# A batch's gate and row-sum rounds gathered in one place, three exponentials a group for four, and a third score buffer

## Chip, core and metric

The kernel runs on one core of one Trainium2 chip. The metric is the device time of one execution in microseconds (us). Five things work side by side: TensorE (PE, matmuls; its weight loads are PEld), VectorE (DVE), ScalarE (ACT), GpSimd (POOL), and SyncE (SP), which here only issues DMA transfers. Each engine takes its instructions strictly in the order in which the program lists them.

## What is computed

Attention with capped scores, and behind it a layer of eight experts to which tokens are assigned greedily:

```python
# q, k, v: 8 batches x 12 heads x 448 x 64, float32; cap = 30
scores = cap * np.tanh(scale * (q @ k.T) / cap)
attn = exp(scores - max); attn = attn / (sum(attn) + 1e-09)
x = (attn @ v), heads side by side: 3584 x 768
logits = x @ w_gate                       # 8 experts, each takes 448 tokens,
...                                       # in order of falling logit
out[mask] = np.maximum(x[mask] @ w1[e], 0.0) @ w2[e]
```

The change lies in the attention alone.

## The kernel before, in words

Attention goes through N = 24 groups, g = 0 to 23. A group is four heads of one batch, so a batch b is three groups, m = 0, 1, 2 with g = 3b + m; they are called G0, G1 and G2 of the batch here. A group has seven rows r = 0 to 6 of key positions. For each row there is

- a score block (`qk`, L148), four matmuls of 64x64 weights and 448 columns into a pair of PSUM banks, which ACT reads with Tanh (L159) into a tile `e`;
- an exponential on the tile of Tanh results, in place (L164). Rows are taken together for it: 0 and 1, 2 and 3, 4 and 5, and 6 alone (`GRP`, L134). It is issued behind the Tanh of the row after its last (`wait`, L161);
- a value block (`avq`, L196), four matmuls that add `e` times the values into the accumulator `psA`, one pair of banks for a whole group. The value blocks of group g run while the score blocks of g+1 do. When all seven are done, DVE copies `psA` into `xT` (`av_out`, L210), and only then may the first value block of the next group write `psA` again.

On the side DVE turns the keys and queries of the next group (`tr`, L133: tiles `tk`, `tq`), adds up a group's exponentials into a tile `es` (`esum`, L170: three adds, a fourth for G2), and turns the attention output of two batches before (`turn`, L271). POOL adds the two halves of `es` for G0 and G1 (`halves`, L356 and L357: a copy of one element, `pin`, which holds it until a certain add of DVE is done, and the add), and scales the turned output by the row sums (`scale`, L278: `xw<-x,R`), which SP then stores. `es` has four buffers, `xw` and `x` two.

For each batch b there are three rounds of small matmuls (`rnd`, L219; 32 rows of result each), which form the gate logits from `xT` and the row sums from `es`, side by side in one bank. They are made for batch b-1 during batch b: R0 in G0, R1 in G1, R2 in G2. Behind R2 DVE copies the banks out (`logit_in`, L256 and L258) and forms the reciprocals of the sums (`sums`, L261 and L262), which POOL spreads into `R` (L264, four copies). In G0 of the next batch PE turns the logits (`ltr`, L290) and DVE finishes them (`logit`, L301 to L309), and POOL adds up the heads (`heads`, L326). In the first batch there are four rounds, since its first group is laid out differently.

The order of all this is written out by hand: the body of the loop over g (L364 to L398) and, for PE, the strings `ORDER`, `EARLY`, `BEFORE` and `FINAL` (L348 to L351), where Q3 is the score block of row 3, A3 the value block of row 3 of the group before. No scheduler reorders it. PSUM has eight banks: two pairs for scores (`psS`), two single banks (`psM`) for rounds, turns and the like, and the pair `psA`.

After the attention come the search for the first expert's tokens and the experts' matmuls, which the change does not touch.

Of the kernel before, what the change touches and what calls it, by code (L numbers as in the profile page):

```python
# [8 lines left out]
PSUM=bass.MemoryType.PSUM  # L9
# [8 lines left out]
def attention(nc, tc, c1, xp, pM, ep, nl, pT, q, k, v, cap, w_gate, xs, L1, ident, on_logits, on_turn, NDEF, setup, mark):  # L18
# [29 lines left out]
    with ExitStack() as ctx:  # L48
# [5 lines left out]
        pS=ctx.enter_context(tc.tile_pool(name="pS",bufs=2,space=PSUM))  # L54

# [31 lines left out]
        ips=pM.tile([128,512],F32,name="psM")  # L87
# [46 lines left out]
        GRP=((0,1),(2,3),(4,5),(6,)); LOC={r:(gi,n) for gi,rs in enumerate(GRP) for n,r in enumerate(rs)}  # L134
# [5 lines left out]
        def qk(g,r):  # L140
            gi,n=LOC[r]
            if n==0: eh[g,gi]=ep.tile([128,len(GRP[gi]),2,S],F32,name=f"e{gi}")
            ps=pS.tile([128,2,512],F32,name="psS")
            if g:
                for o in range(2):
                    for h in range(2):
                        hp=slice(h*64,h*64+64)
                        nc.tensor.matmul(ps[o*64:o*64+64,h,:S],tks[g,0][hp,o,r*64:r*64+64],tks[g,1][hp,o,:],start=True,stop=True)  # L148
            elif r<6:
                o,u=divmod(r,3)  # L150
                for h in range(2):
# [10 lines left out]
            if g==N-1 and gi>=2: e=ev(g,r)  # L162
            elif n<len(GRP[gi])-1: return
            act=lambda: nc.scalar.activation(e,e,AF.Exp,scale=sr[1],bias=bias)  # L164
            if g==N-1 and gi>=2: act()
            else: wait.append(act)
        def esum(g,what):
            if not 0<=g<N: return
            if what=='e1': es_t[g]=es.tile([128,2,2,S],F32,name="es",bufs=4)
            t=es_t[g]; add=lambda o,a,b: nc.vector.tensor_tensor(o,a,b,op=ALU.add)  # L170
            if g==0 and what in ('e1','e2'):
                o=int(what[1])-1
                add(t[:,o],ex(g,o,0),ex(g,o,1)); add(t[:,o],t[:,o],ex(g,o,2))
            elif g==0:
                e=ev(g,6)
                for o in range(2):
                    w=slice(64*(1-o),128-64*o)
                    add(t[w,o],t[w,o],e[w])
# [62 lines left out]
        def logit_v(b,of,t,under):  # L241
# [3 lines left out]
            ps=pM.tile([128,512],F32,name="psM")  # L245
# [113 lines left out]
        def rounds(bb,m,n):  # L359
            rnd(bb,*RNO[bb>0][n])  # L360
            if m==2:
                logit_in(bb)
                if bb<B-NDEF: sums(bb)
        for g in range(N):  # L364
# [7 lines left out]
            order=g>=G2; first=bb==0; old=bb-1 if m==0 and 0<=bb-1<B-NDEF else None  # L372
            qk(g,0)
            if old is not None: ltr(old)
            if m==0 and bb>=0: rounds(bb,m,"R0")
            qk(g,1)
            av_out(g-2)
            if g and (m or g<G2): avq(g-1,0)
# [5 lines left out]
            two=(0,1) if m==1 else (1,0)
            tr(g+1,two[0] if order else 0)
            if order: tr(g+1,two[1])
            if m==1 and bb>0: on_logits(bb-1)
            for w in ('e2','r') if g==1 else ('e2','r6'): esum(g-1,w)
            if g>1 and not HELD(g-1): esum(g-1,'r0')
            if last: halves(N-2,None)  # L390
            if not order: tr(g+1,1)
            for t in (EARLY[g] if g<2 else FINAL if last else BEFORE if g==N-2 else ORDER[m]).split():
                if t[0]=='R': bb>=0 and rounds(bb,m,t)
# [11 lines left out]
        two=pS.tile([128,2,512],F32,name="psS")  # L405
# [22 lines left out]
class Routing:  # L428
# [198 lines left out]
    def search(s,wp,turned=()):  # L627
# [7 lines left out]
        if turned:  # L635
# [3 lines left out]
            post=lambda: s.flips(s.pm.tile([128,512],F32,name="psM"))  # L639
# [461 lines left out]
def full(nc,tc,q,k,v,cap,wg,w1,w2,out):  # L1101
    with ExitStack() as ctx:
# [10 lines left out]
        pM=xctx.enter_context(tc.tile_pool(name="pM",bufs=2,space=PSUM,side="right"))  # L1113
        r.psum=lambda: pM.tile([128,512],F32,name="psM")
# [13 lines left out]
        deferred,tail=attention(nc,tc,cp,xp,pM,ep,nl,pT,q,k,v,cap,wg,xs,L1,ident,on_logits,on_turn,NDEF,(r.indices,r.setup),r.mark)  # L1128
# [37 lines left out]
```

## Time and profile before

| | |
|---|---|
| time, median of 3 runs | 857.54 us (857.45 to 857.86) |
| the profiled execution | 858.0 us, of which its span 856.2 us |
| granted TensorE clock | 0.999 of full speed |
| PE busy | 840.2 us, 98% of the span |
| DVE, ACT, POOL busy | 580.4, 572.4, 462.5 us |
| a batch of the attention in its steady part, mean | 35.39 us |

The profiled execution is one run, recorded by the hardware; its span is the stretch from its first to its last instruction. Busy time is that in which an engine has an instruction under way; a busy PE may still stand still between matmuls, so pauses there are found from the starts of its rows. In rows of the timeline, neighbours of one kind are merged (x24 means 24 records), and a bracket names what ended the idle time ahead of the row. A float32 matmul leaves two records, so a block of four matmuls shows as x8.

### The profile page before, as it was taken

Reading aid. Unit: us, or ns where it says so; the run is one execution under the profiler, and the core shown is the slowest. Engines: PE = TensorE matmul, PEld = TensorE weight load, DVE = VectorE, ACT = ScalarE, POOL = GpSimd, SP = SyncE. Lnnn points to the kernel's source line nnn. Section 1 sums busy time; section 2 is a strip of 40 time slices with the busy share of each in tenths; the row PEclk is TensorE's granted clock in tenths of the full one; section 3 lists DMA queues with packets and bytes.
Section 4 is the critical chain, followed back from the end, with each engine's and each line's share of the span. In section 5 each row is a group of like instructions: output and inputs, shape, how many; then the busy total and the mean of one; then the engine's idle time right before and its main releaser. Section 6 shows DMA issues by size and latency. Waiting matters only on the chain.

```text
span 856.2 us, 17676 instructions
## 1 busy us (share of the span) xinstructions
PE 840.2 (98%) x6109; PEld 614.5 (72%) x6109; DVE 580.4 (68%) x1907; ACT 572.4 (67%) x832; POOL 462.5 (54%) x637
## 2 busy tenths in 40 slices
PE   8999999999999998999999999999999999999997
PEld 5333333333333357889889989989899899999997
DVE  3878899999989778667777777777757780230110
ACT  6999999999999753562764755737727725525521
POOL 8203336346333235573673864856856856837931
PEclk9999999999999999999999999999999999999999
DMA  8999999888995107716706917927928828838601
GB/s 126 137 142 148 157 158 156 159 160 158 154 152 125 23 2 226 229 36 189 222 16 193 311 42 209 317 58 207 308 56 211 288 65 232 257 118 234 202 10 56
DMA packets 364249, 133.70 MB, mean 156 GB/s; under 512 B 290592, under 2 KB 357472, under 8 KB 364160
## 3 DMA queue, kind: packets, MB, share of 16 engines
q1 hardware_dynamic: 354656, 102.27, 55.5%
q0 software_dynamic: 4656, 22.02, 7.5%
q10 hardware_dynamic: 4848, 8.29, 2.9%
q8 instruction: 48, 0.79, 0.4%
q14 instruction: 41, 0.34, 0.1%
HBM read 94.40 MB, written 30.08 MB: 145 GB/s over the span
## 4 chain that ended last, share of the span: by engine, by line
PE 76%; issue 7%; DVE 5%; SPq 5%; DMA 4%; POOL 2%; ACT 1%; POOLq 0%; ACTq 0%; DVEq 0%
PE psH L1002 25%; PE psH L1033 20%; PE psA L196 13%; PE psS L148 12%; SPq L83 3%; PE psM L219 2%; DVE es L170 2%; DMA xg<-xs,idx 1%; DVE cmpD L605 1%; POOL w2l L884 1%; DMA k<-in_k_dram 1%; DMA w1r<-in_moe_w_dram 1%; PE psX L826 1%; PE psM L290 1%; SPq L867 1%
## 5 line engine op out<-in xcount | busy, mean ns | idle before, releaser
L1033 PE MATMUL psH<-w2h,hh 128*128 128x384 f32 x896 | 235.3, 340 | 0.0
L1033 PE MATMUL psH<-w2l,hh 128*128 128x384 f32 x512 | 166.5, 340 | 0.5 <-POOL gap L882 0.5
L1033 PEld LDWEIGHTS psH<-w2h,hh 128*128 128x128 f32 x896 | 161.8, 188 | 0.3
L164 ACT ACTIVATE e<-e,bias 128x1792 f32<-128x1792 f32 (+1 forms) x97 | 158.5, 1636 | 0.1
L159 ACT ACTIVATE e<-psS 128x896 f32<-128x896 f32 x168 | 150.5, 956 | 11.1 <-PE psS L148 7.1
L1002 PE MATMUL psH<-xgh,w1h 128*128 128x448 f32 x384 | 143.2, 373 | 0.3 <-ACT xgh L962 0.3
L1002 PE MATMUL psH<-xgh,w1l 128*128 128x448 f32 x384 | 141.5, 369 | 0.0
L148 PE MATMUL psS<-tq,tk 64*64 64x448 f32 x1288 | 139.3, 538 | 1.1 <-ACT e L159 1.1
L884 POOL TENSOR_TENSOR w2l<-w2r,w2h 128x768 fp32r<-128x768 f32 x64 | 118.1, 1846 | 37.5 <-ACT w2h L880 30.5
L1002 PE MATMUL psH<-xgl,w1h 128*128 128x448 f32 x384 | 136.8, 369 | 0.0
L196 PE MATMUL psA<-e,nv 64*64 64x448 f32 x1232 | 131.9, 539 | 1.0 <-DVE xT L210 1.0
L884 POOL TENSOR_TENSOR w1l<-w1r,w1h 128x768 fp32r<-128x768 f32 x62 | 114.2, 1843 | 19.7 <-ACT w1h L880 15.3
L148 PEld LDWEIGHTS psS<-tq,tk 64*64 64x64 f32 x1288 | 47.5, 132 | 75.4 <-issue 47.0
L196 PEld LDWEIGHTS psA<-e,nv 64*64 64x64 f32 x1232 | 44.8, 133 | 73.8 <-issue 64.3
L1033 PEld LDWEIGHTS psH<-w2l,hh 128*128 128x128 f32 x512 | 95.6, 188 | 1.5 <-POOL gap L882 1.4
L1008 ACT ACTIVATE hh<-psH 128x448 fp32r<-128x448 f32 x64 | 34.8, 544 | 86.4 <-PE psH L1002 80.1
L1010 DVE SCALAR_TENSOR_TENSOR hh<-psH,hh 128x64 fp32r<-128x64 f32 (+1 forms) x128 | 44.0, 386 | 67.8 <-ACT hh L1008 66.7
L1039 ACT ACTIVATE on<-psH 128x384 f32<-128x384 f32 x48 | 23.4, 487 | 88.5 <-PE psH L1033 82.5
L170 DVE TENSOR_TENSOR es<-es,e 128x896 f32<-128x896 f32 (+2 forms) x48 | 77.7, 1619 | 2.5
L909 POOL DMA_INDIRECT xg<-xs,idx x32 | 34.3, 1073 | 81.2 <-DVE zz L774 64.8
L1002 PEld LDWEIGHTS psH<-xgh,w1h 128*128 128x128 f32 x384 | 72.5, 189 | 5.8 <-ACT xgh L962 0.5
L1002 PEld LDWEIGHTS psH<-xgh,w1l 128*128 128x128 f32 x384 | 72.3, 188 | 5.3
(390 smaller groups left out, 1339.1 us busy)
## 6 DMA issues: line engine op xcount, KB each, us to landing
w1r<-in_moe_w_dram SPq DMA_DIRECT2D x128, 192.0 KB, 4.7
w2r<-in_moe_w_dram SPq DMA_DIRECT2D x64, 384.0 KB, 6.5
k<-in_k_dram SPq DMA_DIRECT2D x92, 112.0 KB, 3.8
q<-in_q_dram SPq DMA_DIRECT2D x92, 112.0 KB, 4.0
nv<-in_v_dram SPq DMA_DIRECT2D x88, 112.0 KB, 3.3
xs<-xw SPq DMA_DIRECT2D x72, 112.0 KB, 2.6
xz<-pl ACTq DMA_DIRECT2D x18, 384.0 KB, 3.3
xs<-xn SPq DMA_DIRECT2D x1, 1344.0 KB, 6.5
```

Of the source, the lines that this page charges most:

```text
L83: (nc.scalar if first and a else nc.sync).dma_start(z[w:w+32,lo*NB:hi*NB,:],src[b,h0+2*t+lo:h0+2*t+hi,:,a*32:a*32+32].rearrange("h (k s) d ...
L148: nc.tensor.matmul(ps[o*64:o*64+64,h,:S],tks[g,0][hp,o,r*64:r*64+64],tks[g,1][hp,o,:],start=True,stop=True)
L159: nc.scalar.activation(ev(g,r),ps[:,:,:S],AF.Tanh,scale=sr[0])
L164: act=lambda: nc.scalar.activation(e,e,AF.Exp,scale=sr[1],bias=bias)
L170: t=es_t[g]; add=lambda o,a,b: nc.vector.tensor_tensor(o,a,b,op=ALU.add)
L196: nc.tensor.matmul(avp[g,o][h*64:h*64+64,:S],z[hp,r,h,:],ev(g,r)[hp,h,:],start=r==0,stop=r==6)
L884: (eng or nc.gpsimd).tensor_tensor(view(l),r,view(h).bitcast(F32),op=ALU.subtract)
L909: g=nc.gpsimd.indirect_dma_start(out=row(j,n),out_offset=None,in_=xs,in_offset=bass.IndirectOffsetOnAxis(ap=res[p][0][:n,j:j+1],axis=0))
L1002: nc.tensor.matmul(ps[:,:C],a[:,c,:],b[:,c,:],start=(m==0),stop=(m==DC*3-1)); m+=1
L1008: nc.scalar.activation(h[:,:C],ps[:,:C],AF.Relu)
L1010: nc.vector.scalar_tensor_tensor(h[:,d:d+b-a],ps[:,a:b],0.0,h[:,a:b].bitcast(F32),op0=ALU.max,op1=ALU.subtract)
L1033: nc.tensor.matmul(ps[:,:HD],h[:,f,a:a+128],spl[p,2,hf,f//2][w][:,f%2,:],start=(m==0),stop=(m==nm-1))
```

## The change

1. The exponentials of a group are taken in three parts, rows 0 to 2, 3 and 4, 5 and 6.
2. `es` is summed by five adds of 896 columns (`p`, `q`, `s`: rows 0+1+2 into one half, 3+4+5+6 into the other) in place of two of 1792 and one of 896. The sixth, for G2, joins the halves as before.
3. The three rounds stand together at the end of G1 of the next batch, with `logit_in` and `sums` behind them; `halves` runs in G2 and G0 and no longer in G1 and G2.
4. Scores, rounds, turns and logits share one ring of three pairs of banks (`two_banks`), where there were two pairs for scores and two single banks for the rest.
5. The order is one string a group, in which letters stand for the side work too: c is `av_out`, T `ltr`, l `logit`, t `turn`, `scale` and `tr`, s and a the adds, p the first two adds of the group itself, o the first half of the routing's proposals, i `logit_in` and `sums`. A5- and A6- are value blocks left over from the group before the last.

```diff
+        def two_banks():
+            two_banks.n+=1
+            return pS.tile([128,2,512],F32,name="psS") if two_banks.n%3 else pM.tile([128,2,512],F32,name="psM")
...
-        GRP=((0,1),(2,3),(4,5),(6,)); LOC={r:(gi,n) for gi,rs in enumerate(GRP) for n,r in enumerate(rs)}
+        GRP=((0,1,2),(3,4),(5,6)); LOC={r:(gi,n) for gi,rs in enumerate(GRP) for n,r in enumerate(rs)}
...
-            ps=pS.tile([128,2,512],F32,name="psS")
+            ps=two_banks()
...
-            elif what=='e1': add(t,eh[g,0],eh[g,1])
-            elif what=='e2': add(t,t,eh[g,2])
-            else:
-                r=int(what[1])
-                add(t[:,0],t[:,0],ev(g,r) if r else t[:,1])
+            if what=='p': add(t[:,0],ev(g,0),ev(g,1)); add(t[:,0],t[:,0],ev(g,2))
+            elif what=='q': add(t[:,1],ev(g,3),ev(g,4))
+            elif what=='r': add(t[:,0],t[:,0],t[:,1])
+            else:
+                add(t[:,1],t[:,1],ev(g,5))
+                if g: add(t[:,1],t[:,1],ev(g,6))
...
-                    if b not in bank: bank[b]=pM.tile([128,512],F32,name="psM")
+                    if b not in misc:
+                        two=two_banks()
+                        for o,z in enumerate((misc,side)): z[b]=two[:,o]
...
+        ORDER=["Q0 c T l t s a A0 Q1 Q2 Q3 A1 A2 Q4 A3 Q5 A4 A5 A6 p Q6",
+               "Q0 c t s a o Q1 A0 A1 Q2 Q3 A2 A3 Q4 A4 Q5 R0 R1 R2 p i Q6",
+               "Q0 A5- A6- c t s a Q1 Q2 Q3 A0 A1 Q4 A2 Q5 A3 A4 A5 A6 p Q6"]
...
-            if m: halves(g-4+m,g-1)
+            if m!=1: halves(g-2,g-1)
...
+                elif t=='s':
+                    esum(g-1,'q'); esum(g-1,'s')
+                elif t=='a':
+                    if not HELD(g-1): esum(g-1,'r')
```

What becomes of the order is seen on three engines, each time in the fifth batch. On PE, before, this is the middle of G1, with round R1 between two score blocks and a value block (L148 is a score block, L196 a value block, `e_...` the exponentials it reads, L219 a round):

```order
L196 MATMUL psA<-e_1840,nv 64x448 x4
L148 MATMUL psS<-tq,tk 64x448 x4
L219 MATMUL psM<-xT,gw 32x448 x2
L219 MATMUL psM<-es,ones 32x448 x2
L196 MATMUL psA<-e_1840,nv 64x448 x4
L148 MATMUL psS<-tq,tk 64x448 x8
```

And this is the end of the same G1 in the changed kernel (score blocks are L153 now, value blocks L199, rounds L224), up to the first blocks of G2:

```order
L199 MATMUL psA<-e_1893,nv 64x448 x4
L153 MATMUL psS<-tq,tk 64x448 x4
L224 MATMUL psS<-xT,gw 32x448 x2
L224 MATMUL psS<-es,ones 32x448 x2
L224 MATMUL psS<-xT,gw 32x448 x2
L224 MATMUL psS<-es,ones 32x448 x4
L224 MATMUL psS<-xT,gw 32x448 x2
L153 MATMUL psM<-tq,tk 64x448 x4
L153 MATMUL psS<-tq,tk 64x448 x4
L199 MATMUL psA<-e_1919,nv 64x448 x8
```

All twelve matmuls of the rounds stand in a row now, ahead of the last score block of G1, and the value blocks of rows 5 and 6 (`e_1919`) have moved behind them, into G2.

On DVE, before, this is the stretch from the last adds of G1 through G2 (L210 is the copy of `psA`, L271 and L133 the three transposes, L256 to L262 `logit_in` and `sums`):

```order
L170 TENSOR_TENSOR es<-e_1972,e_2008 128x1792
L210 COPY xT<-psA 128x896
L271 STREAM_TRANSPOSE x_2116<-xT 128x896
L133 STREAM_TRANSPOSE tq<-q 128x896
L133 STREAM_TRANSPOSE tk<-k 128x896
L170 TENSOR_TENSOR es<-es,e_2030 128x1792
L170 TENSOR_TENSOR es<-es,e_2052 128x896
L256 COPY lg<-psM 128x448
L258 TENSOR_TENSOR lg<-lg,psM 64x448
L261 STREAM_TRANSPOSE lgt<-lg 64x448
L262 RECIPROCAL rec<-lgt 64x84
L170 TENSOR_TENSOR es<-e_2089,e_2126 128x1792
```

The same stretch in the changed kernel (adds are L175, the copy of `psA` L213, `logit_in` and `sums` L261 to L267):

```order
L175 TENSOR_TENSOR es<-e_1967 128x896
L175 TENSOR_TENSOR es<-es,e_1967 128x896
L261 COPY lg<-psS 128x448
L263 TENSOR_TENSOR lg<-lg,psS 64x448
L266 STREAM_TRANSPOSE lgt<-lg 64x448
L267 RECIPROCAL rec<-lgt 64x84
L213 COPY xT<-psA 128x896
L276 STREAM_TRANSPOSE x_2114<-xT 128x896
L138 STREAM_TRANSPOSE tq<-q 128x896
L138 STREAM_TRANSPOSE tk<-k 128x896
L175 TENSOR_TENSOR es<-e_2008 128x896
L175 TENSOR_TENSOR es<-es,e_2034 128x896 x2
```

`logit_in` and `sums` have moved ahead of the copy of `psA` and of the transposes, and each long add has become two short ones.

On POOL, before, this is one batch from the `scale` of G0 on (L278 `scale`, L356 and L357 `halves`, L264 the four copies into `R`, L326 `heads`):

```order
L278 TENSOR_TENSOR xw<-x_1879,R_1788 128x14x2x32
L356 COPY pin<-es 1x1
L357 TENSOR_TENSOR es<-es 128x896
L278 TENSOR_TENSOR xw<-x_1998,R_1788 128x14x2x32
L356 COPY pin<-es 1x1
L357 TENSOR_TENSOR es<-es 128x896
L278 TENSOR_TENSOR xw<-x_2116,R_1788 128x14x2x32
L264 COPY R_2167<-rec 32x84 x4
L326 TENSOR_TENSOR lt_2251<-lt_2251 112x4x48
```

In the changed kernel, from the `scale` of G1 on:

```order
L283 TENSOR_TENSOR xw<-x_1976,R_1686 128x14x2x32
L269 COPY R_2064<-rec 32x84 x4
L362 COPY pin<-es 1x1
L363 TENSOR_TENSOR es<-es 128x896
L283 TENSOR_TENSOR xw<-x_2114,R_1686 128x14x2x32
L362 COPY pin<-es 1x1
L363 TENSOR_TENSOR es<-es 128x896
L331 TENSOR_TENSOR lt_2235<-lt_2235 112x4x48
```

The copies into `R` stand ahead of the first `halves` and of the `scale` of G2 now, and the second `halves` (that of G1) ahead of `heads` and of the `scale` of the next G0.

## Rows read from the trace of the kernel before

**Rows 1.** The windows view, five whole batches: busy time of each engine.

```profile
78.83:255.80 176.97, 176.97 (x1825) 66.56 (x1821) 164.95 (x176) 174.84 (x166) 80.58 (x90) 1.00 0.97 156
```

**Rows 2.** The timeline of PE (start, length): first score blocks of batches, one run of blocks.

```profile
78.83 0.93 PE L148 MATMUL psS<-tq,tk 64*64 64x448 f32 x8
...
147.25 2.44 PE L196 MATMUL psA<-e,nv 64*64 64x448 f32 x24
149.50 0.93 PE L148 MATMUL psS<-tq,tk 64*64 64x448 f32 x8
```

**Rows 3.** The timeline of PE, G0 and G1 of the fifth batch: side work.

```profile
150.36 0.65 PE L290 MATMUL psM<-ident,lg 128*112 128x128 f32 x4
150.94 0.57 PE L219 MATMUL psM<-xT,gw 128*32 128x448 f32 x2
...
164.77 0.57 PE L219 MATMUL psM<-xT,gw 128*32 128x448 f32 x2
...
165.66 0.98 PE L196 MATMUL psA<-e,nv 64*64 64x448 f32 x8
```

**Rows 4.** The timeline of DVE, fifth batch, from `logit_in` to G1.

```profile
145.55 0.62 DVE L256 COPY lg<-psM 128x448 f32<-128x448 f32 x1
...
148.23 2.02 DVE L170 TENSOR_TENSOR es<-e,e 128x1792 f32<-128x1792 f32 x1
150.18 1.08 DVE L210 COPY xT<-psA 128x896 f32<-128x896 f32 x1
...
152.10 1.10 DVE L271 STREAM_TRANSPOSE x<-xT 128x896 f32<-128x896 f32 x1
...
155.11 3.71 DVE L170 TENSOR_TENSOR es<-es,e 128x1792 f32<-128x1792 f32 x2
158.86 1.09 DVE L170 TENSOR_TENSOR es<-es 128x896 f32<-128x896 f32 x1
159.87 2.02 DVE L170 TENSOR_TENSOR es<-e,e 128x1792 f32<-128x1792 f32 x1
161.90 1.09 DVE L210 COPY xT<-psA 128x896 f32<-128x896 f32 x1
...
177.49 3.18 DVE L170 TENSOR_TENSOR es<-es,e 128x1792 f32<-128x1792 f32 x2
```

**Rows 5.** The timeline of ACT, fifth batch: exponential, Tanh, short exponential.

```profile
161.04 1.82 ACT L164 ACTIVATE e<-e,bias 128x1792 f32<-128x1792 f32 x1
162.72 0.95 ACT L159 ACTIVATE e<-psS 128x896 f32<-128x896 f32 x1
163.52 1.08 ACT L164 ACTIVATE e<-e,bias 128x896 f32<-128x896 f32 x1
```

**Rows 6.** The timeline of DVE and POOL in G2 of the last batch, two on one memory.

```profile
284.00 1.98 DVE L170 TENSOR_TENSOR es<-es,e 128x1792 f32<-128x1792 f32 x1
286.09 2.42 DVE L170 TENSOR_TENSOR es<-es,e 128x896 f32<-128x896 f32 x1
284.22 3.35 POOL L278 TENSOR_TENSOR xw<-x,R 128x896 f32<-128x896 f32 x1 [11.06 <-issue]
```

**Rows 7.** The timeline of POOL, fifth batch, from the copies into `R` on.

```profile
148.34 2.90 POOL L264 COPY R<-rec 32x84 f32<-32x84 f32 x4 [5.78 <-DVE rec L262]
...
152.33 1.39 POOL L326 TENSOR_TENSOR lt<-lt 112x192 f32<-112x192 f32 x3 [1.09 <-DVE lt L309]
...
154.01 1.74 POOL L278 TENSOR_TENSOR xw<-x,R 128x896 f32<-128x896 f32 x1
...
162.09 2.09 POOL L357 TENSOR_TENSOR es<-es 128x896 f32<-128x896 f32 x1
```

**Rows 8.** The timeline of DVE, then PE, second batch: loads arrive late.

```profile
47.81 1.11 DVE L133 STREAM_TRANSPOSE tq<-q 128x896 f32<-128x896 f32 x1 [3.60 <-DMA q<-in_q_dram]
...
56.00 1.08 DVE L210 COPY xT<-psA 128x896 f32<-128x896 f32 x1
...
57.14 0.98 PE L196 MATMUL psA<-e,nv 64*64 64x448 f32 x8 [0.55 <-DVE xT L210]
```

More of the change, by code (lines that the diff above doesn't have):

```diff
@@ L86, in attention @@
         nc.scalar.activation(tb,ident[:,0:1],AF.Tanh)
-        ips=pM.tile([128,512],F32,name="psM")
+        ips=pT.tile([128,2,512],F32,name="psA",bufs=1)[:,0]
         def idle(n):
@@ L168, in esum @@
             if not 0<=g<N: return
[L169 to L178, printed above, removed]
-            elif what=='e1': add(t,eh[g,0],eh[g,1])
-            elif what=='e2': add(t,t,eh[g,2])
-            else:
-                r=int(what[1])
-                add(t[:,0],t[:,0],ev(g,r) if r else t[:,1])
+            if what=='p': es_t[g]=es.tile([128,2,2,S],F32,name="es",bufs=4)
+            t=es_t[g]; add=lambda o,x,y: nc.vector.tensor_tensor(o,x,y,op=ALU.add)
+            if what=='p': add(t[:,0],ev(g,0),ev(g,1)); add(t[:,0],t[:,0],ev(g,2))
+            elif what=='q': add(t[:,1],ev(g,3),ev(g,4))
+            elif what=='r': add(t[:,0],t[:,0],t[:,1])
+            else:
+                add(t[:,1],t[:,1],ev(g,5))
+                if g: add(t[:,1],t[:,1],ev(g,6))
+                else:
+                    e=ev(g,6)
+                    for o in range(2):
+                        w=slice(64*(1-o),128-64*o)
+                        add(t[w,o],t[w,o],e[w])
         avp={}; pair=[None]
@@ L371, in attention @@
             last=g==N-1
[L372 to L378, printed above, removed]
-            stored()
-            if m: halves(g-4+m,g-1)
-            if old is not None: logit(old); heads(old)
-            if m==0 and bb>1: on_turn(bb-2)
-            turn(b-2,m); scale(b-2,m)
@@ L384, in attention @@
[L384 to L393, printed above, removed]
+            old=bb-1 if m==0 and 0<=bb-1<B-NDEF else None
@@ new lines, in attention @@
+            two=(0,1) if m==1 else (1,0)
+            stored()
+            if m!=1: halves(g-2,g-1)
+            for t in (EARLY[g] if g<G2 else FINAL if last else ORDER[m]).split():
+                if t[0]=='Q': qk(g,int(t[1]))
+                elif t[0]=='A': avq(g-1-(t[-1]=='-'),int(t[1]))
+                elif t[0]=='R': bb>=0 and rnd(bb,*RNO[bb>0][t])
+                elif t=='c': av_out(g-2)
+                elif t=='T': old is not None and ltr(old)
+                elif t=='l':
+                    if old is not None: logit(old); heads(old)
+                    if bb>1: on_turn(bb-2)
+                elif t=='t':
+                    turn(b-2,m); scale(b-2,m)
+                    for part in two: tr(g+1,part)
+                elif t in 'kv': tr(g+1,t=='v')
+                elif t=='s':
+                    esum(g-1,'q'); esum(g-1,'s')
+                elif t=='a':
+                    if not HELD(g-1): esum(g-1,'r')
+                    if last: halves(N-2,None)
+                elif t=='o': bb>0 and on_logits(bb-1)
+                elif t=='i':
+                    if bb>=0:
+                        logit_in(bb)
+                        if bb<B-NDEF: sums(bb)
+                elif t=='p': esum(g,'p')
@@ L404, in attention @@
         LAST=[RA,RB]
-        two=pS.tile([128,2,512],F32,name="psS")
+        two=two_banks()
+        misc[b]=two[:,1]
         part_v(two[:,0],0,1)
```

43 lines of the change are left out of this document (18 added, 25 removed).

## The prediction

> **What bounds the kernel now.** I read the windows view first, then the timelines of PE, ACT, DVE and POOL over one batch. In five steady batches PE is busy all of 176.97 us, ACT 174.84, DVE 164.95, at a granted clock of 1.00 [rows 1]: a batch takes 35.39 us, PE has no free time, ACT lacks 1% of being the bound, DVE 7%.
>
> PE's 35.39 can be added up. A block of four matmuls takes 0.75 (three blocks in 149.50 - 147.25 = 2.25) [rows 2], so the 42 score and value blocks take 31.5. Going over to side work costs 0.11 (150.36 - 149.50 - 0.75), `ltr` 0.58 (150.94 - 150.36), a round 0.89 (165.66 - 164.77), and the block behind it shows 0.98 for 0.93, so 0.05 for going back [rows 2, 3]. G0 pays 0.11 + 0.58 + 0.89 + 0.05 = 1.63 for `ltr` and R0, G1 and G2 1.05 each: 3.73 a batch, 35.2 in all. The reader is to see that PE does not pause here, so a gain must shorten PE's own list, and a loss must make PE wait. What can make it wait is the copy of `psA`: the value block at 57.14 starts 0.06 after that copy ends (56.00 + 1.08), with 0.55 of PE standing still [rows 8].
>
> **The change part by part.** *PE.* Each round holds 0.75 of pure matmul time like a block; the other 0.14 of its 0.89 I count as part of going back. Three rounds in a row cost 0.11 + 3 x 0.75 + 0.14 + 0.05 = 2.55, `ltr` alone 0.11 + 0.58 + 0.05 = 0.74: 3.29 for 3.73, 0.44 saved a batch. PE alone would need 31.5 + 3.29 = 34.8.
>
> *ACT.* A Tanh takes 0.80 (163.52 - 162.72), an exponential of 1792 columns 1.68 (162.72 - 161.04), one of 896 about 0.94 (its 1.08 less the 0.14 by which 1.82 exceeds 1.68) [rows 5]. So 896 more columns cost 0.74, and one of 2688 takes 2.42. A group goes from 11.58 to 7 x 0.80 + 2.42 + 2 x 1.68 = 11.38: 0.20 less. It is hidden, since ACT is not last in a steady batch, nor will be.
>
> *The ring.* Three pairs for scores, less one while a round or `ltr` waits to be read: two at worst, as before. I count it at nothing; the cover is that PE's score blocks come in runs of two or three, and that `logit_in` reads its pair four blocks before the ring needs it.
>
> *DVE's adds.* An add of 896 is followed after 1.01 by one that does not read it (159.87 - 158.86), and after its own 1.09 and 0.04 by one that does (158.86 against 155.11 + 3.71): 1.13 [rows 4]. Before, the adds of a group take 3.18 and 1.95 (150.18 - 148.23); now p takes 1.13 + 1.01 = 2.14 and the three of s 1.13 + 1.13 + 1.01 = 3.27, with a fourth in G0 4.40. That is 0.3 more a group, 0.9 a batch, which DVE's 7% would hide.
>
> *POOL beside DVE.* At 284.22 `scale` starts while an add runs (284.00 to 285.98); it shows 3.35 where others show 1.74, so it began at about 285.9. The add that came next at 286.09 shows 2.42, and ends 0.94 after `scale` does [rows 6, 7]. In G0 the pair of adds at 155.11 shows 3.71 instead of 3.18, with `scale` running until 155.75 [rows 4, 7]. So an add that arrives during a POOL add waits until that ends, less 0.1, and the other way about; transposes and the copy of `psA` do not. The Trainium skill says so too (SBUF — State Buffer, section "SBUF: two separate sides"): a VectorE instruction with two SBUF inputs and a GpSimd one that reads SBUF exclude each other, and the first to start keeps the ports for its whole length. The trace agrees with it (0.53 and 1.33 us of such waiting); by the page `halves` and the copies into `R` hold adds off as well, the sum below would be the same, and a case without these waits would be less likely.
>
> *DVE's loop.* This is what I think decides. In the changed G1 the first add of p writes the `es` buffer of four groups before, which R0 reads, and R0 now stands almost last in G1. From R0's end DVE's list runs without slack until PE waits for it, round to the next R0:
>
> - p 2.14, `logit_in` and `sums` 2.68 (148.23 - 145.55) [rows 4]: 4.82
> - G2: copy 1.00, the three transposes 3.01 (155.11 - 152.10): 8.83. POOL meanwhile does, from `sums` on, the copies into `R` (1.0 of their 2.90 lie behind the add that held them, 148.34 + 2.90 - 150.25; I take 1.2), `halves` 2.09 and its `pin` (2.25) and `scale` 1.74 [rows 7]: 5.2 against DVE's 4.0, so the add waits 1.1: 9.9
> - s 3.27, p 2.14: 15.3
> - G0: copy and `logit` 1.92 (152.10 - 150.18), transposes 3.01: 20.2. POOL since p: `halves` 2.25, `heads` 1.68 (154.01 - 152.33), `scale` 1.74: 5.7 against 4.9, wait 0.75: 21.0
> - s with r 4.40, p 2.14, the copy 1.08 and 0.06: 28.7. Now A0 of G1 may start
> - PE: nine blocks 6.76 to the first round, R0 0.11 + 0.95 and 0.1 to DVE: 36.6
>
> So a batch takes 36.6, and PE stands still 1.8 of it, at A0 of G0 and A0 of G1. The wait for each POOL piece is not shown in this place: it lies between nothing and a whole `scale`, 1.74; I take 0.75 and 1.1, what the lengths leave over.
>
> *The first batches.* The queries of group 4 land at 47.8, and DVE waits for them [rows 8]; loads are issued as before. Behind that stand, as before, two transposes (1.99), and then s with r and p, 6.54, and the copy: A0 of group 4 at 47.81 + 1.99 + 6.54 + 1.14 = 57.5 instead of 57.14, although PE comes there sooner. From there to the third batch PE needed 78.83 - 57.14 = 21.69 with R1 and R2 (2.10) in it; now all four rounds of the first batch lie there, 4 x 0.75 + 0.30 = 3.30. That is 22.9, so the third batch starts 1.5 late, at 80.4.
>
> *Sum.* The third batch starts with DVE in time: only A0 of G1 is late, by 0.8 (`logit` may start at 1.5, and 0.92 + 3.01 + 0.4 + 4.40 + 2.14 + 1.14 later is 13.5, where PE would be at 12.8): 35.7. Four batches at 36.6 and 0.3 for a routing turn that one of them holds on DVE: 146.7. Together 182.4 against 176.97, +5.4, and +1.5 from the start: +6.9. The last batch I count as even: one visit to side work less (0.3) and the wait for logits gone, against adds that hold up its final copies; a microsecond either way. What follows runs at its own pace and moves as a whole. The profiled execution would take 858.0 + 6.9 = 864.9; against the median, 857.54, it is **864.4 us**.
>
> **Rivals.** *No waits between DVE and POOL, or covered ones.* The loop is then 34.75, and what is left is A0 of G1 behind `ltr` and `logit`, 0.45: a batch takes 35.3, as now, and with the start's 1.5 the time is 857.54 + 1.5 - 0.5 = 858.5, no change. For it: the order of POOL is another, and starts a little earlier or later remove a wait. Against: both waits follow from work that POOL gets from DVE's own instructions, so they travel with it.
>
> *PE's shorter list shows.* DVE's copies are always in time, a batch takes 34.8 (5 x 0.59 = 2.9 less), and the first batch saves its 0.6: 854.0, faster. It decides once DVE's loop is under 34.8 and `logit` no longer follows `ltr` by a microsecond, that is, if some 2 us of what I laid end to end overlaps. Against it: each length is a row's step, with overlap in it already.
>
> *The waits in full.* `scale` has to wait for its buffer's store, comes after the first add of s, and takes the memory between two adds: each wait is a whole 1.74, 0.65 to 1.0 more. At half of that in both places, four to five batches: 868.
>
> **Numbers.** The loop as laid out 0.60 (861 to 867); no change 0.17; faster 0.10; the heavier case 0.13. Within 0.2%, 1.7 us, a measurement of this kernel can hardly tell a time from no change. Faster by more 0.11, within 0.16, slower 0.73. The range, 858 to 869, reaches from the case of no change to the heavier one.
>
> **What would show it.** In the changed profile: batches of 36 to 37 us from the fourth on; PE idle before its value blocks (L199), released by DVE's `xT` (L213), some 1.7 a batch; DVE idle before the adds (L175) behind PE's rounds in G1, and adds of 2 us for 1.09 beside `scale`; DVE busy over 95%, ACT no longer near full; three rounds in some 2.4 us. Wrong would be: batches near 35, the first adds of s in G0 and G2 at 1.09, or copies of `psA` that end before PE asks.

## The result, and the profile after

The changed kernel takes 868.88 us (median of four: 867.96, 868.04, 869.72, 869.95), the kernel before 857.70 in the same comparison: a ratio of 1.013, 95% interval 1.0112 to 1.0147. Forecast were 864.4 and a range of 858 to 869. The median lies 0.12 under the top of the range, two of the four executions lie above it, and the loss is 11.2 us where 6.9 were forecast. The profiled execution took 869.95, its span is 868.2, 12.0 more than before.

From the page, the chain that ended last and PE's value blocks (busy time and mean of one, then idle time ahead of them and what ended it), first of before, then of the changed kernel:

```profile
PE 76%; issue 7%; DVE 5%; SPq 5%; DMA 4%; POOL 2%; ACT 1%; POOLq 0%; ACTq 0%; DVEq 0%
...
L196 PE MATMUL psA<-e,nv 64*64 64x448 f32 x1232 | 131.9, 539 | 1.0 <-DVE xT L210 1.0
```

```profile
PE 57%; DVE 15%; SPq 9%; issue 8%; DMA 8%; POOL 2%; ACT 1%; POOLq 0%; DVEq 0%
...
L199 PE MATMUL psA<-e,nv 64*64 64x448 f32 x1232 | 132.6, 542 | 12.0 <-DVE xT L213 12.0
```

PE waits 12.0 us for the copy of `psA`, where it waited 1.0, and DVE's share of the chain has grown from 5% to 15%. The windows view, in the columns of [rows 1]: the third batch, then four batches.

```profile
82.57:118.41 35.84, 35.09 (x368) 13.62 (x364) 32.35 (x35) 34.63 (x30) 11.66 (x14) 1.00 1.07 157
118.41:266.27 147.86, 140.87 (x1461) 54.49 (x1457) 139.94 (x170) 139.24 (x120) 54.48 (x74) 1.00 1.03 158
```

PE, busy throughout before, lacks 7.0 us in the four batches. DVE and PE are now busy alike, 95%, ACT 94%. The timeline of PE where `ltr` starts, one row a batch, and at the first value blocks of G0 and G1, with the rounds between:

```profile
83.43 0.65 PE L295 MATMUL psM<-ident,lg 128*112 128x128 f32 x4
...
119.28 0.65 PE L295 MATMUL psS<-ident,lg 128*112 128x128 f32 x4
...
156.09 0.65 PE L295 MATMUL psS<-ident,lg 128*112 128x128 f32 x4
...
157.57 0.98 PE L199 MATMUL psA<-e,nv 64*64 64x448 f32 x8 [0.84 <-DVE xT L213]
...
169.89 1.74 PE L199 MATMUL psA<-e,nv 64*64 64x448 f32 x16 [0.81 <-DVE xT L213]
...
176.82 0.57 PE L224 MATMUL psS<-xT,gw 128*32 128x448 f32 x2
...
179.21 0.98 PE L153 MATMUL psM<-tq,tk 64*64 64x448 f32 x8
...
192.90 0.65 PE L295 MATMUL psM<-ident,lg 128*112 128x128 f32 x4
```

Two batches of 36.81, in the second of which PE stands still 0.84 and 0.81; the three rounds take 2.39 (179.21 - 176.82). These signs are as forecast, and so are the adds at 186.88 and 198.18 below; only DVE's share, 94.6%, stays just short of the 95% named. By the starts of `ltr` the 12.0 us are these:

| stretch | before | after | difference | forecast |
|---|---|---|---|---|
| start to `ltr` of the third batch | 79.70 | 83.43 | +3.73 | +1.5 |
| third batch | 35.30 | 35.85 | +0.55 | +0.3 |
| fourth and fifth | 70.66 | 73.62 | +2.96 | +2.4 |
| sixth and seventh | 71.01 | 74.24 | +3.23 | +2.7 |
| last batch, to the first matmul of the search (L826, now L831) | 48.39 | 49.90 | +1.51 | 0 |
| the rest | 551.1 | 551.2 | 0 | 0 |

DVE's loop, as its timeline shows it from the first add of p behind R0 in the fifth batch to the copy ahead of A0 of G1 in the sixth:

```profile
177.91 1.09 DVE L175 TENSOR_TENSOR es<-e 128x896 f32<-128x896 f32 x1 [1.78 <-PE psS L224]
...
182.73 1.09 DVE L213 COPY xT<-psA 128x896 f32<-128x896 f32 x1
...
186.88 2.00 DVE L175 TENSOR_TENSOR es<-e 128x896 f32<-128x896 f32 x1
...
193.25 1.08 DVE L213 COPY xT<-psA 128x896 f32<-128x896 f32 x1
...
195.17 1.10 DVE L276 STREAM_TRANSPOSE x<-xT 128x896 f32<-128x896 f32 x1
...
198.18 1.84 DVE L175 TENSOR_TENSOR es<-e 128x896 f32<-128x896 f32 x1
...
205.58 1.08 DVE L213 COPY xT<-psA 128x896 f32<-128x896 f32 x1
```

And POOL in G2 of the fifth batch, what the add at 186.88 stood against:

```profile
182.83 1.12 POOL L269 COPY R<-rec 32x84 f32<-32x84 f32 x4 [10.17 <-DVE rec L267]
...
184.15 2.10 POOL L363 TENSOR_TENSOR es<-es 128x896 f32<-128x896 f32 x1
186.21 1.71 POOL L283 TENSOR_TENSOR xw<-x,R 128x896 f32<-128x896 f32 x1
```

Term by term, forecast and measured: from the start of R0 to p 1.05 and 1.09; p with `logit_in` and `sums` 4.82 and 4.82; G2's copy and transposes 4.01 and 4.15; the wait beside `scale` 1.1 and 0.91 (2.00 - 1.09); s and p 5.41 and 5.46; copy and `logit` 1.92 and 1.92; transposes 3.01 and 3.01; the second wait 0.75 and 0.75; s with r, p 6.54 and 6.65; copy to A0 1.14 and 1.14; PE to the next R0 6.87 and 6.92. The sum is 36.8 where 36.6 was forecast.

The early loss lies elsewhere. The timelines of DVE and PE (an answer each) and the windows of PE (length, busy, granted clock, DMA share, GB/s), where [rows 8] stood before:

```profile
48.27 1.11 DVE L138 STREAM_TRANSPOSE tq<-q 128x896 f32<-128x896 f32 x1 [3.79 <-DMA q<-in_q_dram]
...
54.72 1.08 DVE L175 TENSOR_TENSOR es<-e 128x896 f32<-128x896 f32 x1
...
56.85 1.08 DVE L213 COPY xT<-psA 128x896 f32<-128x896 f32 x1
...
57.98 2.78 PE L199 MATMUL psA<-e,nv 64*64 64x448 f32 x16 [1.94 <-DVE xT L213]
...
62.74 1.68 PE L199 MATMUL psA<-e,nv 64*64 64x448 f32 x16
```

```profile
56.00:58.00 2.00, 0.06 (x7) 1.00 0.67 129
58.00:60.00 2.00, 2.00 (x16) 0.63 0.65 140
60.00:62.00 2.00, 2.00 (x16) 0.51 1.12 171
```

A0 of group 4 starts at 57.98, 0.48 behind the forecast 57.5, since the queries landed 0.46 later. But PE had stood still for 1.94 us, and then the granted clock fell to half, 1.2 GHz: four blocks took 4.76 (62.74 - 57.98), where four take 3.01 at full clock. Those 1.75 us the forecast did not have.

### The profile page after: what moved, and what is told of

The parts are those of the page before. It is cut to its first block, busy times and chain, and to the rows that moved or that the text cites. A ratio compares the mean times of both kernels' runs of the same rounds, so it can differ in the third digit from the quotient of the medians.

```text
span 868.2 us, 17706 instructions
## 1 busy us (share of the span) xinstructions
PE 840.8 (97%) x6109; PEld 618.9 (71%) x6109; DVE 591.3 (68%) x1950; ACT 569.9 (66%) x808; POOL 446.7 (51%) x637
## 4 chain that ended last, share of the span: by engine, by line
PE 57%; DVE 15%; SPq 9%; issue 8%; DMA 8%; POOL 2%; ACT 1%; POOLq 0%; DVEq 0%
PE psH L1007 23%; PE psH L1038 20%; DVE es L175 6%; PE psA L199 5%; SPq L88 5%; PE psS L153 3%; DMA q<-in_q_dram 2%; DMA xg<-xs,idx 2%; DMA k<-in_k_dram 2%; DVE xT L213 1%; SPq L72 1%; PE psM L153 1%; DVE x L276 1%; DVE cmpD L610 1%; DVE tk L138 1%
## 5 line engine op out<-in xcount | busy, mean ns | idle before, releaser
L169 ACT ACTIVATE e<-e,bias 128x1792 f32<-128x1792 f32 (+2 forms) x73 | 148.2, 2031 | 0.1
L199 PE MATMUL psA<-e,nv 64*64 64x448 f32 x1232 | 132.6, 542 | 12.0 <-DVE xT L213 12.0
L889 POOL TENSOR_TENSOR w2l<-w2r,w2h 128x768 fp32r<-128x768 f32 x64 | 118.1, 1847 | 38.1 <-ACT w2h L885 23.6
L164 ACT ACTIVATE e<-psS 128x896 f32<-128x896 f32 x113 | 101.5, 927 | 17.5 <-PE psS L153 12.1
L199 PEld LDWEIGHTS psA<-e,nv 64*64 64x64 f32 x1232 | 45.5, 133 | 82.0 <-issue 61.5
L153 PE MATMUL psS<-tq,tk 64*64 64x448 f32 x864 | 98.2, 541 | 1.3 <-ACT e L164 1.3
L1013 ACT ACTIVATE hh<-psH 128x448 fp32r<-128x448 f32 x64 | 34.8, 544 | 86.6 <-PE psH L1007 80.1
L175 DVE TENSOR_TENSOR es<-es,e 128x896 f32<-128x896 f32 (+1 forms) x70 | 77.8, 1111 | 4.0
L1007 PEld LDWEIGHTS psH<-xgl,w1h 128*128 128x128 f32 x384 | 72.3, 189 | 5.2
```

The costliest lines, as they stand in the source:

```text
L175: t=es_t[g]; add=lambda o,x,y: nc.vector.tensor_tensor(o,x,y,op=ALU.add)
L199: nc.tensor.matmul(avp[g,o][h*64:h*64+64,:S],z[hp,r,h,:],ev(g,r)[hp,h,:],start=r==0,stop=r==6)
L889: (eng or nc.gpsimd).tensor_tensor(view(l),r,view(h).bitcast(F32),op=ALU.subtract)
L1007: nc.tensor.matmul(ps[:,:C],a[:,c,:],b[:,c,:],start=(m==0),stop=(m==DC*3-1)); m+=1
L1013: nc.scalar.activation(h[:,:C],ps[:,:C],AF.Relu)
```

## Experiments

The kernel before ran beside each, with medians of 858.1 to 859.5 us; kernels are compared by their ratios to it.

**POOL's order (e1_pool).** `halves` of G0 moves into G1, ahead of the copies into `R`; `heads` moves behind `scale`.

```diff
-            if m!=1: halves(g-2,g-1)
+            if m==0 or g<G2: halves(g-2,g-1) if m!=1 else None
...
-                    if old is not None: logit(old); heads(old)
+                    if old is not None: logit(old)
...
                     turn(b-2,m); scale(b-2,m)
+                    if old is not None: heads(old)
...
                     if bb>=0:
+                        halves(g-1,g)
                         logit_in(bb)
```

> The changed kernel with POOL's order altered: the add of halves of G0 is issued in G1 ahead of the copies into R, so that it runs beside logit_in and sums, and heads stands behind scale. No work is left out. Theory (DVE's loop with waits at the memory that it shares with POOL): the first adds of s take 1.1 us in G0 and G2 where they took 1.83 and 2.00, a batch falls from 36.8 to about 35.2, over four and a half batches 7 us: 862 us. Rival (the waits only fill time in which DVE would wait for ACT or PE anyway): batches stay at 36.8 and the time at 868 to 870.

Measured: 864.07 us (863.01 to 866.38), ratio 1.0073 (1.006 to 1.0087). The timelines of DVE and PE, the first adds of s in G0 and G2 and A0 of G1:

```profile
157.09 1.40 DVE L175 TENSOR_TENSOR es<-e 128x896 f32<-128x896 f32 x1
...
182.19 1.05 DVE L175 TENSOR_TENSOR es<-e 128x896 f32<-128x896 f32 x1
...
165.20 1.73 PE L199 MATMUL psA<-e,nv 64*64 64x448 f32 x16 [0.65 <-DVE xT L213]
```

The wait is gone in G2 and down to 0.3 in G0, PE no longer stands still at A0 of G0, and a batch takes 35.78 (188.21 - 116.66 = 71.55 for two). So the waits at the shared memory were on the path. The ratio is 0.57% (4.9 us) lower, but not all of that need be POOL's order: of the 6.9 us between the two profiled executions 2.5 lie ahead of the third batch (`ltr` at 80.91 for 83.43), where the queries landed at 47.45, PE stood still 1.27 at A0 of group 4 and the clock stayed at 1.00. From the fourth batch on, all but the seventh are about 1 us shorter. The theory's 35.2 a batch and 862 us were not reached: the other pause, A0 of G1, stays at 0.65 to 0.78, and DVE now waits 0.20 for `ltr` ahead of `logit` (at 188.90).

**The copy in group 4 (e2_copy).** The adds p of group 3 move behind the copy of `psA`, there alone (in the code `G2` is the number 3, the first group of the second batch).

```diff
                 elif t=='c':
                     av_out(g-2)
+                    if g==G2+1: esum(g-1,'p')
...
-                elif t=='p': esum(g,'p')
+                elif t=='p': g!=G2 and esum(g,'p')
```

> The changed kernel with one move in group 4 alone: the first two adds of group 3 stand behind the copy of psA instead of ahead of it. Theory (the early loss is that copy's lateness, and the granted clock that falls after PE has stood still for it): A0 of group 4 at 54.9 instead of 57.98, no stretch at half the clock, ltr of the third batch at 79.7 instead of 83.43, the time 865.2 us, and the two levels of the runs (868.0 and 869.8) become one. Rival (the queries that land late hold the first batches, and the wait only moves to the next copy): ltr at 82.5 or later, 868 us.

Measured: 866.31 us (865.80 to 866.81), ratio 1.0093 (1.0078 to 1.0108); `ltr` of the third batch at 79.06. DVE's timeline, then PE's windows:

```profile
54.17 1.08 DVE L213 COPY xT<-psA 128x896 f32<-128x896 f32 x1
```

```profile
56.00:58.00 2.00, 2.00 (x26) 1.00 0.49 100
58.00:60.00 2.00, 2.00 (x28) 1.00 0.88 177
```

No pause and no fall of the clock; the start is even a little earlier than before (79.70; 0.7 of what it gains on the changed kernel lies ahead of group 4). It gives back 3.8 us of span in the profiled executions (868.2 to 864.4), 0.37% or 3.2 us by the ratios. Of the changed kernel's four executions two are 1.9 and 2.0 us shorter than the profiled one, with a mean granted clock of 0.999 for its 0.998, while the four of this kernel lie within 1.0: as if the fall came in some only. That fits, but only one of the changed kernel's executions has a trace.

**Exponentials in four parts again (e3_four)**, on the changed kernel.

```diff
-        GRP=((0,1,2),(3,4),(5,6))
+        GRP=((0,1),(2,3),(4,5),(6,))
```

> The changed kernel with the exponentials in four parts a group again, all else as changed. Theory (ACT is not what a batch waits for): ACT's busy time 4 to 5 us more over the attention, batches 36.8 as before, the time 868.9 within 1 us. Rival (waiting for three Tanhs before the first exponential holds up the value blocks or the adds): 3 us or more faster.

Measured: 876.85 us (875.47 to 878.33), ratio 1.0211 (1.0198 to 1.0224): 0.8% slower than the changed kernel, which neither theory had. ACT's and PE's timelines in G2 of the fifth batch:

```profile
183.89 1.78 ACT L169 ACTIVATE e<-e,bias 128x1792 f32<-128x1792 f32 x1
185.56 0.91 ACT L164 ACTIVATE e<-psS 128x896 f32<-128x896 f32 x1
186.36 1.04 ACT L169 ACTIVATE e<-e,bias 128x896 f32<-128x896 f32 x1
...
186.53 0.98 PE L153 MATMUL psS<-tq,tk 64*64 64x448 f32 x8 [1.26 <-ACT e L164]
```

With four parts the exponential of rows 4 and 5 (183.89) falls between Tanhs that PE's order wants close together; a score block then waits for its pair of banks. In the early stretch the pause at A0 of group 4 grows to 2.96 (the queries landed 0.53 later than in the changed kernel), and the clock is at 0.58 from 58 to 62. In the steady batches of the changed kernel PE waits for ACT once, 1.32 in the sixth; with four parts it does so in most.

**The rounds two blocks earlier (e4_rounds)**, to free p.

```diff
-               "Q0 c t s a o Q1 A0 A1 Q2 Q3 A2 A3 Q4 A4 Q5 R0 R1 R2 p i Q6",
+               "Q0 c t s a o Q1 A0 A1 Q2 Q3 A2 A3 Q4 R0 R1 R2 A4 Q5 p i Q6",
```

> The changed kernel with the three rounds two blocks earlier in G1, ahead of A4 and Q5. Theory (p's first add waits for R0, and this wait is part of the loop): DVE's wait ahead of p falls from 1.78 to about 0.3, a batch from 36.8 to 35.4, the time to 862.5 us. Rival 1 (the wait moves: R1 then waits on PE for the joined halves of G2, or p for its exponential): batches at 36.5 or more, 867 us or more. Rival 2 (what holds PE is not DVE's loop but its own list with three rounds in a row): 868 to 870.

Measured: 876.51 us, ratio 1.0215 (1.0202 to 1.0228); one of six executions took 1398.99 us, at a mean granted clock of 0.556 where the others have 0.993 to 0.997; the ratio leaves it out, and why its clock was low is not known. ACT's timeline:

```profile
181.59 0.92 ACT L164 ACTIVATE e<-psS 128x896 f32<-128x896 f32 x1 [2.11 <-PE psS L153]
```

p no longer waits for R0 (0.49 for its exponential, as rival 1 had it), but ACT gets no scores while PE does three rounds and A4, 2.11 us, which takes up all that ACT had to spare in a batch of the changed kernel (147.86 - 139.24 over four, 2.15); at the start of G2 of the fourth batch, where DVE had the proposals, PE stands still for 2.77. The place of the rounds is what feeds ACT.

**POOL's order and the copy in every G1 (e5_both).** As the first experiment, and p of G0 behind the copy in all batches from the second on.

```diff
                     av_out(g-2)
+                    if g>G2 and m==1: esum(g-1,'p')
...
-                elif t=='p': esum(g,'p')
+                elif t=='p': (g<G2 or m) and esum(g,'p')
```

> POOL's order as in e1_pool, and in G1 of every batch from the second on the first two adds of G0 behind the copy of psA instead of ahead of it. Theory (what is left of the loss after e1_pool is the copy that frees psA for A0 of G1, 0.65 to 0.73 us a batch and 1.27 in group 4, because DVE does p first): no PE idle before A0 of G1, a batch falls from 35.8 to 35.0, the time from 864 to 859 or 860 us. Rival (DVE's loop has no slack left, and the lateness turns up at the next wait, R0 to p or A0 of G0): batches at 35.6 to 35.8, 862 to 864 us.

Measured: 858.44 us (857.32 to 859.22) beside 859.47 of before, ratio 0.9984 (0.9975 to 0.9993). The changed kernel's loss is gone, and 0.16% won. What PE still waits for between the second batch and the last (its timeline, all such rows):

```profile
139.68 0.98 PE L153 MATMUL psM<-tq,tk 64*64 64x448 f32 x8 [1.02 <-DVE lg L263]
151.66 0.98 PE L199 MATMUL psA<-e,nv 64*64 64x448 f32 x8 [0.48 <-DVE xT L213]
...
212.45 0.98 PE L153 MATMUL psS<-tq,tk 64*64 64x448 f32 x8 [1.34 <-ACT e L164]
```

They stand in the fourth and the sixth batch, in which the routing's proposals go to DVE ahead of p, and at the first value block behind the fourth. The third batch takes 34.86 and the seventh 34.92, which is PE's own list as forecast (34.8).

**The copy in every G1 alone (e10_copy)**, POOL's order as changed (the diff is the one above).

> The changed kernel with only the second move of e5_both: the adds of G0 behind the copy of psA in G1, POOL's order as changed. Theory (two waits a batch, of separate causes): no PE idle at A0 of G1, 0.83 us still at A0 of G0 with the add beside scale there and in G2, a batch 36.0, the time 861.5 us. Rival (one loop, so that cutting it in one place is enough, or so that the wait at A0 of G0 grows by what the other lost): batches at 35.0 and 859 us, or at 36.8 and 866 us as in e2_copy.

Measured: 862.02 us (861.09 to 862.87), ratio 1.0035 (1.0021 to 1.0048). In the main as the theory had it: no pause at A0 of G1, and one still at A0 of G0, of 0.82 or 0.83 in the fourth, sixth and last batch, but of 1.44 and 1.40 in the fifth and seventh, behind the batches with proposals; batches of 36.3 to 36.4 for the 36.0 expected. Of the changed kernel's ratio POOL's order alone takes 0.57%, the copies alone 0.95% (group 4's among them), both together 1.46%: nearly the sum of the two, though the first holds some of the early stretch. Curing one wait does not cure the other.

**Two pairs for scores (e6_ring2).** The third pair serves rounds, `ltr` and turns alone.

```diff
         def two_banks():
-            two_banks.n+=1
-            return pS.tile([128,2,512],F32,name="psS") if two_banks.n%3 else pM.tile([128,2,512],F32,name="psM")
+            return pM.tile([128,2,512],F32,name="psM")
...
-            ps=two_banks()
+            ps=pS.tile([128,2,512],F32,name="psS")
```

> The changed kernel with two pairs of banks for scores alone, and the third pair for rounds, ltr and the like alone, in the same order. Theory as predicted (the ring of three is worth nothing): 868.9 us within 1.5, score blocks do not wait for Tanhs. Rival (e3_four and e4_rounds showed score blocks that wait for ACT: the order needs the third pair): PE idle before score blocks behind ACT, 872 us or more.

Measured: 881.09 us (878.17 to 882.24), ratio 1.0242 (1.0224 to 1.0261). A batch takes 37.28, `ltr` of the third starts at 87.64, and score blocks wait for Tanh all over (PE's timeline):

```profile
153.01 0.98 PE L150 MATMUL psS<-tq,tk 64*64 64x448 f32 x8 [0.57 <-ACT e L161]
```

The third pair, forecast at nothing, is worth 1.1% to this order, about 10 us.

**The rounds in their old places (e7_apart)** as well, with two single banks beside two pairs for scores.

```diff
-        ORDER=["Q0 c T l t s a A0 Q1 Q2 Q3 A1 A2 Q4 A3 Q5 A4 A5 A6 p Q6",
-               "Q0 c t s a o Q1 A0 A1 Q2 Q3 A2 A3 Q4 A4 Q5 R0 R1 R2 p i Q6",
-               "Q0 A5- A6- c t s a Q1 Q2 Q3 A0 A1 Q4 A2 Q5 A3 A4 A5 A6 p Q6"]
+        ORDER=["Q0 c T R0 l t s a A0 Q1 Q2 Q3 A1 A2 Q4 A3 Q5 A4 A5 A6 p Q6",
+               "Q0 c t s a o Q1 A0 A1 Q2 R1 Q3 A2 A3 Q4 A4 Q5 p Q6",
+               "Q0 A5- A6- c t s a Q1 Q2 R2 i Q3 A0 A1 Q4 A2 Q5 A3 A4 A5 A6 p Q6"]
...
```

The banks and the last group change with it: that group's string takes R2 as well, and the values are turned in two goes again.

> The changed kernel with the rounds back in their places of before (R0 in G0 behind ltr, R1 in G1, R2 and logit_in in G2), two pairs of banks for scores and two single banks for the rest; exponentials, adds and the order of all else as changed. Theory (DVE is held to a loop because R0 stands late in G1 and p waits for it): no DVE wait ahead of p, batches at 35.3 to 35.8 although adds still wait beside scale, 861 to 863 us. Rival (the adds and the waits at the memory fill DVE by themselves, with the rounds anywhere): batches at 36.5 or more, 867 us or more.

Measured: 887.36 us (884.92 to 888.54), ratio 1.0321 (1.0305 to 1.0338), batches of 38.1. It does not tell the theories apart: with two pairs for scores PE waits for ACT at four places a batch (0.28 to 0.61 us), and DVE is not what is waited for. The rounds apart with three pairs were not tried; a pair held from G0 to G2 leaves no third one.

**Three parts alone, on the kernel before (e8_three).**

```diff
-        GRP=((0,1),(2,3),(4,5),(6,))
+        GRP=((0,1,2),(3,4),(5,6))
...
-            elif what=='e1': add(t,eh[g,0],eh[g,1])
-            elif what=='e2': add(t,t,eh[g,2])
+            elif what=='e1': add(t[:,0],ev(g,0),ev(g,1)); add(t[:,0],t[:,0],ev(g,2))
+            elif what=='e2': add(t[:,1],ev(g,3),ev(g,4)); add(t[:,1],t[:,1],ev(g,5))
+            elif what=='r6': add(t[:,1],t[:,1],ev(g,6))
```

> The kernel before with exponentials in three parts and the five adds of 896, all else as before. Theory (both are hidden where PE never waits): the time of before within 1 us, batches at 35.3. Rival 1 (ACT's 0.2 us a group shows): 855 us or less. Rival 2 (DVE's 0.3 us a group, or the longer first exponential, holds up PE): 860 us or more.

Measured: 884.66 us (883.31 to 885.16), ratio 1.029 (1.0276 to 1.0304), 25 us: rival 2, far beyond its bound. ACT's and PE's timelines:

```profile
144.43 2.53 ACT L164 ACTIVATE e<-e,bias 128x2688 f32<-128x2688 f32 x1
146.85 1.71 ACT L159 ACTIVATE e<-psS 128x896 f32<-128x896 f32 x2
...
147.81 0.98 PE L148 MATMUL psS<-tq,tk 64*64 64x448 f32 x8 [1.26 <-ACT e L159]
```

While ACT is in the long exponential, PE has filled both pairs; it waits until the Tanh behind it frees one. A batch takes 38.72. Such a wait for ACT is what the third pair spares the changed kernel, but for the one of 1.32; whether a third pair alone would have cured the order of before was not tried.

**The remaining waits of DVE (e9_all).** As e5_both, with p behind the copy in groups 2 and 3 too, the proposals behind `logit_in` and `sums`, and the turn of the values ahead of s in the last group.

```diff
-               "Q0 c t s a o Q1 A0 A1 Q2 Q3 A2 A3 Q4 A4 Q5 R0 R1 R2 p i Q6",
+               "Q0 c t s a Q1 A0 A1 Q2 Q3 A2 A3 Q4 A4 Q5 R0 R1 R2 p i o Q6",
...
-        FINAL="Q0 A5- A6- c t Q1 s a Q2 A0 Q3 V A1 Q4 L A2 Q5 A3 W Q6 A4 A5 A6"
+        FINAL="Q0 A5- A6- c t V Q1 s a Q2 A0 Q3 A1 Q4 L A2 Q5 A3 W Q6 A4 A5 A6"
...
-                    if g>G2 and m==1: esum(g-1,'p')
+                    if g in (2,3) or g>G2 and m==1: esum(g-1,'p')
...
-                elif t=='p': (g<G2 or m) and esum(g,'p')
+                elif t=='p': g in (1,2) or g>=G2 and m==0 or esum(g,'p')
```

> e5_both with three more moves: the first two adds also behind the copy of psA in groups 2 and 3; the routing's proposals in G1 behind logit_in and sums instead of ahead of p; in the last group the turn of the values ahead of the adds s. Theory (each of the waits that e5_both's profile still shows for DVE is one of order): the 1.27 and 0.70 us of PE idle in groups 2 and 3, the 1.02 and 0.48 in the batch with proposals and the 0.91 in the last group go, 4 us in all: 854 to 855 us when before takes 858. Rival (queries and keys of the first groups land when they land, and the time won there is lost again; the other moves only shift a wait): 857 to 858 us.

Measured: 857.40 us (856.58 to 859.21) beside 858.95, ratio 0.9983 (0.9974 to 0.9992): no more than e5_both, so the rival. The waits of 1.02 and of 0.91 in the last group are gone from their places, but PE's timeline shows the proposals' wait in a new place:

```profile
143.41 1.73 PE L199 MATMUL psA<-e,nv 64*64 64x448 f32 x16 [1.28 <-DVE xT L213]
```

**The same without the move of the proposals (e11_best).**

> e9_all without the move of the proposals, which in e9_all only moved the wait to A0 of G2 and of the next G0 (1.28 and 0.35 us). Theory (the moves in groups 2 and 3 and of the turn of the values are worth 1.5 and 0.9 us, where the first stretch runs at full clock): 1 to 2 us under e5_both, a ratio to before of 0.997. Rival (ACT is the next bound: what PE wins early it waits for ACT): a ratio of 0.9985, as e5_both and e9_all.

Measured: 857.64 us (854.74 to 859.85) beside 858.11, ratio 0.9991 (0.9977 to 1.0005). What was won in groups 2 and 3 is lost again at the queries of group 4 (timelines of DVE and PE):

```profile
48.48 1.11 DVE L138 STREAM_TRANSPOSE tq<-q 128x896 f32<-128x896 f32 x1 [3.23 <-DMA q<-in_q_dram]
...
56.05 1.73 PE L199 MATMUL psA<-e,nv 64*64 64x448 f32 x16 [1.17 <-DVE xT L213]
```

`ltr` of the third batch starts at 79.80 there, 79.39 in e5_both. The theory's gain does not show, and what stands in its way is the queries' landing, not ACT as the rival had it. The three versions can't be told apart; against before they are level or up to 0.2% faster.

## Why the prediction was right, and what was mis-sized

*The time* is in the range by 0.12 us, and that is luck in part: the early stretch and the last batch took 3.7 us that the sum did not have, and they fit only because the range left room for heavier waits at the shared memory, which did not come.

*DVE's loop* was right in place, order and size: 36.81 a batch for 36.6, with both of PE's pauses (1.65 together for 1.8) where they were put. The two moves that cut it, of POOL's order and of the copy, gave back 1.46% where 1.3% had been lost. *The waits beside POOL* were 0.91 and 0.75 for 1.1 and 0.75. The Trainium skill (SBUF — State Buffer, section "SBUF: two separate sides") has the first to start keep the ports for its whole instruction. The add at 186.88, held until `scale` was done at 187.92 less 0.1, agrees with it, and so does the e1_pool kernel, where `scale` of G2 was through before the add came.

*The first batches* are the term that was mis-sized: 3.73 for 1.5. The lateness of A0 of group 4 and the rounds that move into this stretch were counted; that a pause of 1.94 halves the clock behind it was not, though the working had PE there "sooner" and so had the pause in it. 1.75 of the 2.2 missing are that, 0.46 the queries' landing, which lies between 47.45 (e1_pool) and 48.80 (e3_four) in the profiled runs that wait for it. *The last batch*, counted as even, lost 1.5: the loop still runs in it, and PE stands still at A0 of its G0 and G1 as in the batches ahead. Besides, the seven columns of values are turned in one go, and a score block waits 0.91 for that copy, which stands on DVE behind adds that `scale` holds up (301.49, L235). The two pauses are what the loss hangs on: e5_both, without them but with the wait of 0.91, takes 47.95 from `ltr` to the search, less than before. *The sixth and seventh batch* lost 3.23 for 2.7, but not as laid out: the sixth takes 38.38, with a score block in its G2 that waits 1.32 for a Tanh (a wait that is gone in e9_all, where the proposals stand elsewhere), and the seventh 35.86, with no pause at A0 of G0. That the two nearly make the forecast is chance. PE's timeline, the sixth and the last batch:

```profile
221.35 0.98 PE L153 MATMUL psS<-tq,tk 64*64 64x448 f32 x8 [1.32 <-ACT e L164]
...
268.62 0.98 PE L199 MATMUL psA<-e,nv 64*64 64x448 f32 x8 [0.83 <-DVE xT L213]
...
280.95 1.74 PE L199 MATMUL psA<-e,nv 64*64 64x448 f32 x16 [0.82 <-DVE xT L213]
```

*The rival of waits in full*, 868, has the time that was measured, and is wrong all the same: no wait in the steady batches was a whole 1.74. *PE's shorter list* did show once DVE was out of the way (34.86 for 34.8). It took both moves of order to get there.

*ACT's 0.20, called hidden, and the ring at nothing* do no harm to the sum, and are wrong as statements on the parts. (ACT's busy time fell by 0.16 a batch, 34.97 to 34.81, where 0.20 a group would be 0.6.) Three exponentials and the short adds in the order of before, with its two pairs, cost 2.9%; the changed order loses 1.1% more without its third pair, and 0.8% more with four exponentials. The cover named for the ring (score blocks in runs of two or three) was not there with two pairs, where score blocks wait 0.28 to 0.58 for Tanh. The sum came out because the change makes these parts together.

What stays open: whether the rounds could stand apart at no cost beside three score pairs, whether the two levels of the changed kernel's times (868.0 and 869.8) are the clock's fall, and how the proposals come to hold up a score block in the sixth batch.

## What to carry to other kernels

Follow an engine's list round until it meets itself: DVE was busy 93% before and in the steady batches never waited for, but the move of the rounds closed a loop through PE in which 1.7 us of waits at the shared memory and two adds ahead of a copy had no cover left. When an accumulator's copy gates the next engine, issue it ahead of work that nobody waits for yet; that, and POOL's pieces in the order of their inputs, turned a loss of 1.3% into a gain of 0.16% with the same work. Price the parts of a change together: a longer exponential, a third buffer and an order that needs both can each look free or ruinous alone.

## What the runs showed of the hardware

The granted clock fell to half behind pauses of PE of 1.94 us (changed kernel), 2.01 (e8_three), 2.25 (e6_ring2), 2.77 (e4_rounds), 2.10 and 2.96 (e3_four). It stayed at 1.00 behind one of 1.96 (e6_ring2, ends at 45.75), behind one of 3.05 (e7_apart, ends at 311.94), and behind a second one of 2.77 in e4_rounds. The windows of PE in that kernel, behind its pauses that end at 144.63 and at 295.86:

```profile
144.00:146.00 2.00, 1.37 (x8) 0.60 1.44 154
146.00:148.00 2.00, 2.00 (x16) 0.55 1.53 148
...
295.00:297.00 2.00, 1.14 (x12) 1.00 0.00 0
297.00:299.00 2.00, 2.00 (x28) 1.00 0.00 0
```

So the length of a pause alone does not tell whether its price is paid once or nearly twice. The Trainium skill (TensorE: Matmul & The Clock Gate, section "HAM oscillation — how this bites in real kernels") tells of matmul stages that run at half clock behind a wait for data. The trace agrees with the effect, here behind waits for a copy and for ACT, at a price of 1.75 us for the pause of 1.94.
